# Score and state products cut into 32-row column tiles, with a new recorded order of the whole program

## The chip, the cores and the metric

The kernel runs on one core of one Trainium2 chip. The metric is the device time in microseconds (us) of one execution of the program. The kernel before takes 615.61 us, the median of 3 runs (615.38 to 616.79).

## The reference

Two stages stand one behind the other. The first is a linear recurrence over 768 time steps for 4 batches and 8 heads of width 48, with a complex decay per step and row; the second is a feed-forward network (FFN) over 3072 tokens, with a rational function between its two products. Cut to its core:

```python
mag = np.sqrt(a_re * a_re + a_im * a_im)
scale = np.minimum(mag, 0.999) / (mag + 1e-06)
a_re_n, a_im_n = (a_re * scale, a_im * scale)
for t in range(S):                                   # S = 768
    S_re, S_im = ar * S_re - ai * S_im + kv, ar * S_im + ai * S_re
    y[:, :, t] = np.einsum('bhd,bhde->bhe', q[:, :, t], S_re)
...
h = x @ w_in                                         # 3072 x 384 times 384 x 2048
P = a[0] + a[1] * h + a[2] * h2 + a[3] * h3
Q = 1.0 + np.abs(b[0]) * np.abs(h) + np.abs(b[1]) * h2
return ((P / (Q + 1e-06)) @ w_out).astype(np.float32)
```

Here kv is the outer product of row t of k and v, and h2, h3 are powers of h.

## The kernel before, in words

The recurrence is computed by chunks. Time is cut into 6 chunks of 128 steps; a unit is one chunk of one batch, so there are 24 units, taken in 12 pairs. For a unit, VectorE, ScalarE and GpSimd turn the decays into scaled rows of q and k (`norm`, `angle`, `trig`, `outer`): the last step there multiplies QK by the cosines (tile CO) and the sines (tile T) into two tiles Q, and a DMA through SyncE's queue then lays Q out as HQ, 96 rows for each head (48 real, 48 imaginary), with q in the first half and k in the second. Two HQ tiles take turns.

TensorE then does four things for a unit (`attn`). It transposes the k half (line 597). It multiplies k by q for each head, 128 x 128 scores over 96 rows (L608), four heads to a PSUM bank; VectorE multiplies them with a triangular mask into ST. It multiplies ST by V and the running state St by q (L624); these outputs have 32 rows each and use the array as four column tiles of 32 columns. And it updates the state from kT and V: in chunks 0 to 2 by eight products of 96 rows and 48 columns (L642), in chunks 3 and 4 by eight turned products with V's columns as rows (L653), whose result ScalarE evacuates, a DMA shifts, four transposes turn back (L663), and VectorE adds. The last chunk has no state to update. All banks of this stage come from a ring of two, `at`.

The FFN follows by tiles of 512 columns in `ph`: 96 of them, the first product at L704 and the second, into `po`, at L720. The first two pairs of units use plain float32 weights (4 bytes, two passes on TensorE for each product); all later ones use weights split into a high and a low part (wiH and wi, wh and wo), with three products for each. Between the two products stand some five operations each of ScalarE (Abs, Square, a reciprocal root) and VectorE, and a last one on VectorE or GpSimd (g). The weights come in as raw 8-byte numbers and are folded to float32 by VectorE, ScalarE and GpSimd at the start.

What runs when is not left to a scheduler at build time. Every operation is put into a plan, and a table, `ORDER`, holds a number for each of them: which operation comes next in the program, and on which engine it runs where there is a choice. So many multiplies may stand on VectorE or on GpSimd (lists `EN`, `DP`), and ScalarE's order says how often its function tables change between the sines and the FFN's functions. The planner's prices (`MM512`, the number ahead of each `pe` call) serve the search for an order; with a recorded one they have no effect on the program.

Until the first pair is there, `rouse` puts products on the idle array (L676), into a bank that nobody reads.

Of the kernel before, what the change touches and what calls it, by code (L numbers as in the profile page):

```python
# [221 lines left out]
def act(n, psum=False):  # L222
# [7 lines left out]
    "c-m!Hd3;XS+Fd8}AlW-ewP`ECt(I0P(*97ThKPCUH3db@LlE;&)I1XvgqA2Su9+f+nunXBt!injl9+qZ?2{PsW;)Ne&dc}v{`mfQUvKt4XYXfNYdy~c@I@G2"  # L230
    "MUjLcgx?qC6m|tIedfc}ClZDz{2}hI%CK-xo~p|BJ+Y7{K6n%Vl^jHiEni`3^!=<FT)ix{@T0sNQ!YDQUXQt(^%}BKT2j$h^7K0<5aTgLlF>{@n>9#MzuIq!"
    "Mv|Uud=QQYa#hz-yKlvp{DMPjvUwHx;)jRwhvca+<lDuvMS5bdJd_R58Ce@KLn<OG+AsS&>PDZ>j+G$%M9XY6RK+F?R!mQOsVPJ6{BT^JB2LcB6J6K5fnD+z"
    "F6iAd-$diCl;-{c^|9RvyQ7QD2~!I}F$vixC108&Jvu*Y7p^lVY0?{YVd;~m6l&<xrVfV6QeB*TqolpQVlJ!w#uqbiMr}6zbxk`_!eUCYHlZ47$`eUpL|S66"
    "DsPw4p~x^DaFKq@k`8Da-8;Jt4ob01;P*3C%dRg&u}|7*$JEw;iO#Fwq)QS{c`V^EU9-pNYo?9NL4JgP&OO;9&!jVIR{StCR(hd1MoK*2ZG{-0ys+)&F4vkd"
    "cbUvoQyi6lNgBW7(L;I6P&|`3ebh9CuRdhHR;TPEGG7W+u-%Qh>80|sGW2TG6HTQ^BG3_Mr7r%(UmjIxdg-+$!pbXuG&@0N;jBtC;nq&+j{iC*&=#Mms<y~j"
    "ER;!j<b+$vGEA0WILhL-a}b@eO>WcIZWUT*c7%e**@)KBem8@$QO>B@D)MH5?4Vy8qPy5TRbh5s`BmAo5Q;>Z%G1_h0j@h`tvPbrTIqC<SY6&8gd7RR-{n_i"
    "Pe5MyYq^hQj#xTTHOQ{)bIf@p_rs%dA32fMJ*S#=!-=pSI_3F^vF1uYqJ5d_XScPwI6kN+)vQ#xB=ZrBF;WGiF-->Jq#Pou3Zxvd-jgexWGU7V%dcS!Dq3Tm"
    "NW>FgDe8N>v3!a&8HFXp%{kO2s>)%bUQfg?CMKuw`%@fI*G-D`r(<EM%s>Nlm0;c4p3gh~_TEyv!i~)Ja$jaf+{xK1ooL@m3DIrrAgq&ds7-6q<d#%mK6XoA"
    "td@?*a2i?bWB_c5L{x=a5|H(PeEI;VWu2^JW<&6WOvGH70!?&G!+Ke)dfSW<R;j-BQ@)kN$X2wbg%7k#<a3!{AtiGlUa9aX)5r2e`()L@r_tYJpC=2WEA-Ah"
    "fSxMT?8HqOMJtBkbH?QoF*QM!;UwleOR=1OJyF3Z<Qqj&$jlT-0DKUH5)pYyB)-mjTFN$bN0h9=W$8+G{U`;PD)ZHwb}-(-R`n129WwbpnC>jXWcu0xw<TRE"  # L240
    "yF0G(-c;4g<mlJ!1Cl^YT8xiJeECFqD#(}UC5Poc8j))=l_QS4p4&t!VHLR?i$SWFT?yHI+DHb*GMd#;345eEu5kaVG+-QiU@H;$2~Rq!I+<3Cn}-ZONXzf)"
# [31 lines left out]


@with_exitstack
def attn_moe(ctx: ExitStack, tc: tile.TileContext, qk, aa, v, w_in, w_out, coef, heads, lanes, out):
    nc = tc.nc
    cst = ctx.enter_context(tc.tile_pool(name="cst", bufs=1))
    fast = ExitStack()
# [4 lines left out]


    ident = cst.tile([P, P], F32R, name="ident")
    cmask = cst.tile([P, P], F32, name="cmask")
    make_identity(nc, cmask)
    nc.scalar.activation(ident, cmask, AF.Copy)
    nc.gpsimd.memset(cmask, 0.25)  # L290
# [817 lines left out]
```

## Time and profile before

| | |
|---|---|
| median of the runs | 615.61 us |
| span of the profiled execution, first to last instruction | 612.9 us |
| TensorE products (PE) busy | 563.6 us, 92% |
| TensorE weight loads (PEld) busy | 482.3 us, 79% |
| VectorE (DVE) busy | 566.4 us, 92% |
| ScalarE (ACT) busy | 515.3 us, 84% |
| GpSimd (POOL) busy | 213.0 us, 35% |

The span is that of one profiled execution, the only time that the profile gives for it; the runs' median stands 2.7 us above it. Busy time counts a product from its start to its modelled end; since products are pipelined, their price is better read from one start to the next.

### The profile page before, as it was taken

Reading aid. Unit: us, or ns where it says so; the run is one execution under the profiler, and the core shown is the slowest. Engines: PE = TensorE matmul, PEld = TensorE weight load, DVE = VectorE, ACT = ScalarE, POOL = GpSimd, SP = SyncE. Lnnn points to the kernel's source line nnn. Section 1 sums busy time; section 2 is a strip of 40 time slices with the busy share of each in tenths; the row PEclk is TensorE's granted clock in tenths of the full one; section 3 lists DMA queues with packets and bytes.
Section 4 is the critical chain, followed back from the end, with each engine's and each line's share of the span. In section 5 each row is a group of like instructions: output and inputs, shape, how many; then the busy total and the mean of one; then the engine's idle time right before and its main releaser. Section 6 shows DMA issues by size and latency. Waiting matters only on the chain.

```text
span 612.9 us, 12009 instructions
## 1 busy us (share of the span) xinstructions
PE 563.6 (92%) x4454; PEld 482.3 (79%) x4454; DVE 566.4 (92%) x953; ACT 515.3 (84%) x867; POOL 213.0 (35%) x212
## 2 busy tenths in 40 slices
PE   0059999999999999999999999999999999999995
PEld 0038788888999999998878877878888888878874
DVE  8999999999999999999989999999999999778884
ACT  7979999999789889979988978989968877478781
POOL 2535346364536433515334133333520250000100
PEclk9999999999999999999999999999999999999999
DMA  8889632535573265155054255371423232010001
GB/s 286 312 218 314 141 96 69 133 100 140 104 155 102 46 126 135 53 105 129 6 138 104 64 123 116 97 164 19 101 78 113 54 63 32 1 52 1 1 2 56
DMA packets 40193, 63.57 MB, mean 104 GB/s; under 512 B 4544, under 2 KB 26176, under 8 KB 40128
## 3 DMA queue, kind: packets, MB, share of 16 engines
q1 hardware_dynamic: 39552, 62.08, 40.2%
q10 hardware_dynamic: 576, 0.66, 0.6%
q8 instruction: 37, 0.61, 0.4%
q14 instruction: 28, 0.23, 0.1%
HBM read 37.75 MB, written 4.72 MB: 69 GB/s over the span
## 4 chain that ended last, share of the span: by engine, by line
PE 49%; DVE 24%; ACT 14%; DMA 6%; issue 5%; SPq 1%; DVEq 0%; ACTq 0%
PE po L720 19%; PE ph L704 19%; DVE Af L336 5%; ACT Zf L351 4%; PE at L608 4%; PE at L624 4%; DVE g L336 4%; DVE T L336 3%; DVE ph L336 2%; DVE Q L336 2%; ACT Af L351 2%; DMA HQ<-Q 2%; PE at L597 1%; DVE MM L336 1%; DMA g<-in_w_out 1%
## 5 line engine op out<-in xcount | busy, mean ns | idle before, releaser
L720 PE MATMUL po<-g,wh 128*128 128x512 f32 (+1 forms) x576 | 167.2, 360 | 0.0
L704 PE MATMUL ph<-X,wiH 128*128 128x512 f32 (+1 forms) x576 | 144.2, 365 | 1.9 <-DVE Af L336 1.6
L720 PE MATMUL po<-g,wo 128*128 128x256 f32 (+1 forms) x462 | 141.2, 367 | 0.0
L720 PEld LDWEIGHTS po<-g,wh 128*128 128x128 f32 x576 | 102.9, 189 | 17.0 <-issue 1.2
L704 PEld LDWEIGHTS ph<-X,wiH 128*128 128x128 f32 x576 | 96.3, 188 | 21.2 <-DVE Af L336 2.9
L720 PEld LDWEIGHTS po<-g,wo 128*128 128x128 f32 x462 | 86.5, 189 | 12.1 <-issue 0.6
L336 POOL TENSOR_TENSOR g<-Af,Zf 128x512 fp32r<-128x512 f32 x31 | 42.4, 1366 | 148.2 <-DVE Af L336 63.9
L336 DVE SCALAR_TENSOR_TENSOR ph<-Zf,co,ph 128x512 f32<-128x512 f32 x96 | 71.8, 748 | 7.0 <-ACT Zf L351 3.8
L351 ACT ACTIVATE Zf<-ph,co 128x512 f32<-128x512 f32 x96 | 65.3, 680 | 14.6 <-DVE g L336 7.0
L351 ACT ACTIVATE Zf<-Af,co 128x512 f32<-128x512 f32 x80 | 57.8, 722 | 22.5 <-DVE ph L336 20.8
L336 DVE SCALAR_TENSOR_TENSOR g<-ph,co,Zf 128x512 fp32r<-128x512 f32 x80 | 59.5, 744 | 15.3 <-ACT Zf L351 14.6
L351 ACT ACTIVATE Af<-Af,co 128x512 f32<-128x512 f32 x96 | 68.8, 720 | 1.1
L704 PE MATMUL ph<-X,wi 128*128 128x512 f32 (+1 forms) x264 | 67.3, 358 | 0.0
L336 DVE SCALAR_TENSOR_TENSOR Af<-Af,co,g 128x512 f32<-128x512 f32 x80 | 64.7, 809 | 2.0
L351 ACT ACTIVATE Af<-ph 128x512 f32<-128x512 f32 x96 | 56.4, 589 | 8.0 <-PE ph L704 7.9
L336 DVE SCALAR_TENSOR_TENSOR Af<-ph,co,Af 128x512 f32<-128x512 f32 x80 | 59.7, 747 | 1.5
L704 PEld LDWEIGHTS ph<-X,wi 128*128 128x128 f32 x264 | 45.8, 188 | 8.1
L351 ACT ACTIVATE Zf<-Zf 128x512 f32<-128x512 f32 x80 | 50.3, 629 | 1.8
L608 PE MATMUL at<-HQ 96*128 96x128 f32 x384 | 49.5, 276 | 0.6 <-ACT kT L342 0.6
L608 PEld LDWEIGHTS at<-HQ 96*128 96x128 f32 x384 | 47.5, 191 | 2.9 <-ACT kT L342 1.3
L704 PE MATMUL ph<-wh,wi 128*128 128x256 f32 x192 | 45.0, 383 | 1.6 <-DVE g L336 1.6
L676 PE MATMUL po<-Q,cmask 128*128 128x256 f32 x28 | 10.0, 472 | 37.7 <-DVE Q L336 35.9
(213 smaller groups left out, 1053.9 us busy)
## 6 DMA issues: line engine op xcount, KB each, us to landing
HQ<-Q SPq DMA_DIRECT2D x141, 128.0 KB, 4.7
AA<-in_aa SPq DMA_DIRECT2D x23, 384.0 KB, 3.9
QK<-in_qk SPq DMA_DIRECT2D x23, 384.0 KB, 4.3
V<-in_v SPq DMA_DIRECT2D x24, 256.0 KB, 4.2
g<-in_w_in SPq DMA_DIRECT2D x6, 512.0 KB, 6.5
wh<-in_w_in SPq DMA_DIRECT2D x6, 512.0 KB, 5.8
wh<-in_w_out SPq DMA_DIRECT2D x8, 384.0 KB, 4.3
g<-in_w_out SPq DMA_DIRECT2D x8, 384.0 KB, 5.8
```

Of the source, the lines that this page charges most:

```text
L336: call = lambda e: getattr(e, kind)(*map(real, args), **{k: real(x) for k, x in kw.items()})
L351: e.activation(o(), i(), f, **kw)
L597: e.transpose(pt[:, i].bitcast(F32R), hq[:, 4 * g + i, 1, :], ident)
L608: e.matmul(pst[:, i, :], hf[:, 4 * g + i, 1, :], hf[:, 4 * g + i, 0, :], start=True, stop=True)
L624: e.matmul(py[32 * y:32 * y + 32, min(j, 2), :], l, sts[h // 4][:, h % 4, :] if q is None else hf[:, h, 0, :], start=q is None and j == 0, ...
L676: plan.op(dict(PE=(430, lambda e, x=x: e.matmul(idle[:, 0:2 * C], cmask, x(), start=True, stop=True)), SP=(0, lambda e: None)), (w,), ((id ...
L704: e.matmul(o, wt[f // 4 * NJ + j][:, f % 4 * P:f % 4 * P + P], moving(j, hl), start=n == 0, stop=n == len(prods) - 1)
L720: e.matmul(o[:, cols], wt[:, j * P:j * P + P], gg, start=(f == 0 and n == 0 and cols.start == 0), stop=(f == NFF - 1 and n == len(prods) - ...
```

## The change

Four things are changed. The scores of a head are no longer one product of 128 x 128, but four strips of 32 rows of k, each only with the columns of q from its first row on; heads are taken in pairs, and the odd head's strips lie in the bank in reverse order (`STRIPS`). The mask becomes one of two halves, in bfloat16, and V's odd heads have their blocks of 32 rows reversed on the host, so V has a second copy of these heads in plain order for the state. The state update is the same for all chunks: three products of 32 rows and 48 columns for each head; the turned products, their evacuation, DMA and transposes are gone. The two `at` banks are named outright. And there is another `ORDER`, with 32 warming products instead of 18 kept in it. Some planner prices differ too. `vn` serves a fallback path that does not run here.

```diff
-MM512 = 231.5
+MM512 = 236.5
-TURNED = 3
+VPAIR = VP + D
+VROW = H // 2 * (VPAIR + D)
+STRIPS = ((0, 1), (1, 2), (0, 0), (1, 3), (1, 1), (0, 2), (1, 0), (0, 3))
+def vcol(h):
+    return h // 2 * VPAIR + h % 2 * VP
 ORDER = (
-    "c-m!Hd3;XS+Fd8}AlW-ewP`ECt(I0P(*97ThKPCUH3db@LlE;&)I1XvgqA2Su9+f+nunXBt!injl9+qZ?2{PsW;)Ne&dc}v{`mfQUvKt4XYXfNYdy~c@I@G2"
+    "c-l=^33!#&ng0HpeIfq|1cyb*1;rN7I<_KJc%UON0t3n-7Qxg4VJGa1M3E&aAOWGsB0?ZQ0TqNs1)(ULBDS5WBLRnMAr}w?3OOf9$wIjQJMTFOoq6t)-20z<"
...
+    cmask = eye.bitcast(BF16).rearrange("p (y t) -> p y t", y=2)
...
+    banks = [ps.tile([P, 512], F32, name=f"at{i}") for i in range(2)]
...
-        u.V = V = buf(wk, [P, H * VP], F32, "V", VB)
+        u.V = V = buf(wk, [P, VROW], F32, "V", VB)
...
             def scores(e, g=g, pst=pst):
-                for i in range(4):
-                    e.matmul(pst[:, i, :], hf[:, 4 * g + i, 1, :], hf[:, 4 * g + i, 0, :], start=True, stop=True)
-
-            pe(870, scores, u.hq, (pst,))
+                for i in (0, 2):
+                    for y, q in STRIPS:
+                        h, s0 = 4 * g + i + y, 32 * (3 - q if y else q)
+                        e.matmul(pst[32 * q:32 * q + 32, i + y, s0:C], hf[:, h, 1, s0:s0 + 32], hf[:, h, 0, s0:C], start=True, stop=True)
+
+            pe(585, scores, u.hq, (pst,))
...
-        if c < TURNED:
-            def states(e):
-                for h in range(H):
-                    e.matmul(pd[0:96, h], kT[:, h], V[:, VP * h:VP * h + D], start=True, stop=True)
-            pe(1303, states, (V, kT), (pd,))
...
-            def turned(e):
-                for h in range(H):
-                    y, m = ((0, VP), (VP, D))[h % 2]
-                    e.matmul(pd[y:y + m, h // 2], V[:, VP * h:VP * h + m], kT[:, h], start=True, stop=True)
...
+        def states(e):
+            for h in range(H):
+                n = H // 2 * VPAIR + h // 2 * D if h % 2 else vcol(h)
+                for m in range(0, 2 * D, 32):
+                    e.matmul(pd[m:m + 32, h], kT[:, h, m:m + 32], V[:, n:n + D], start=True, stop=True)
+
+        pe(680, states, (V, kT), (pd,))
...
-                plan.op(dict(PE=(430, lambda e, x=x: e.matmul(idle[:, 0:2 * C], cmask, x(), start=True, stop=True)),
+                plan.op(dict(PE=(430, lambda e, x=x: e.matmul(idle[:, 0:2 * C], ident.bitcast(F32), x(), start=True, stop=True)),
```

TensorE's order at the scores of a unit, in the FFN's stretch of full 512-column tiles; a row's shape is weight columns x streamed columns. Before, eight heads stand between first-layer products:

```order
L704 MATMUL ph<-X_92,wiH_1070 128x512
L704 MATMUL ph<-X_92,wiH_229 128x512
L608 MATMUL at<-HQ_88 128x128 x8
L704 MATMUL ph<-X_92,wiH_348 128x512
L704 MATMUL ph<-X_92,wiH_1070 128x512
```

After, at a unit in the same place of the program, the last strips of such a stretch:

```order
L623 MATMUL at_112<-HQ_95 32x96 x2
L623 MATMUL at_112<-HQ_95 32x128 x2
L623 MATMUL at_112<-HQ_95 32x64 x2
L623 MATMUL at_112<-HQ_95 32x32 x2
L700 MATMUL ph<-X_99,wiH_310 128x512
L700 MATMUL ph<-X_99,wiH_337 128x512
```

Four full products of a group have become sixteen strips, and the stretch between full products is now one in column tiles.

The same engine at a state update. Before, in chunk 2, between first-layer products:

```order
L704 MATMUL ph<-X_92,wiH_1070 128x512
L704 MATMUL ph<-X_92,wiH_229 128x512
L642 MATMUL at<-V,kT 96x48 x8
L704 MATMUL ph<-X_92,wiH_348 128x512
L704 MATMUL ph<-X_92,wiH_1070 128x512
```

After, between products of the second layer and the first:

```order
L716 MATMUL po_3713<-g,wo-1_1196 128x512
L716 MATMUL po_3713<-g,wh_786 128x512
L661 MATMUL at_111<-V,kT 32x48 x24
L700 MATMUL ph<-X_99,wiH_334 128x512
L700 MATMUL ph<-X_99,wiH_374 128x512
```

Eight products of 96 weight columns are now twenty-four of 32, again a stretch of their own in column tiles.

GpSimd's order, some 115 instructions into its program, where units of the second and third chunk are prepared. Before:

```order
L336 TENSOR_TENSOR g<-Af,Zf 128x512
L336 TENSOR_TENSOR RU<-MM,RU 128x3x128
L336 TENSOR_TENSOR g<-Af,Zf 128x512
L336 COPY ncar<-MM 128x3
L336 TENSOR_TENSOR QK<-QK,RU 128x768
L336 TENSOR_SCALAR MM<-SQ 128x384
```

After:

```order
L350 TENSOR_TENSOR Q<-QK,T 128x768
L350 TENSOR_TENSOR RU<-MM,RU 128x3x128
L350 COPY ncar<-MM 128x3
L350 TENSOR_TENSOR QK<-QK,RU 128x768
L350 TENSOR_TENSOR Q<-QK,CO 128x768
L350 TENSOR_TENSOR wo_2485<-wo_676,wh_1816 128x384
```

Multiplies of 768 columns that VectorE did before (Q from QK and the sines or cosines) now stand on GpSimd, in the chain that ends in HQ.

## Rows read from the trace of the kernel before

**Rows 1.** The page: busy time by engine; busy tenths in 40 slices of 15.3 us.
```profile
PE 563.6 (92%) x4454; PEld 482.3 (79%) x4454; DVE 566.4 (92%) x953; ACT 515.3 (84%) x867; POOL 213.0 (35%) x212
...
PE   0059999999999999999999999999999999999995
...
DVE  8999999999999999999989999999999999778884
```

**Rows 2.** Waits of TensorE: who waited for whom, us in all, times, longest.
```profile
PE po L676 <- DVE Q L336: 35.9, 1, 35.9
PE ph L704 <- DVE g L336: 1.6, 2, 1.2
...
PE at L597 <- DMA HQ<-Q: 0.3, 1, 0.3
```

**Rows 3.** Table by stretch: length, busy us (instructions) by engine, PE clock, DMA share, GB/s.
```profile
60.00:120.00 60.00, 58.48 (x367) 50.91 (x365) 59.29 (x105) 57.94 (x101) 26.49 (x32) 1.00 0.47 117
240.00:300.00 60.00, 60.00 (x596) 55.00 (x595) 58.24 (x99) 54.47 (x94) 23.54 (x23) 1.00 0.34 77
480.00:540.00 60.00, 60.00 (x443) 49.11 (x442) 49.87 (x79) 42.03 (x68) 13.29 (x9) 1.00 0.22 38
```

**Rows 4.** Timeline of TensorE, 333 to 341 us: start, us, line, out<-in, rows*columns, shape, count.
```profile
333.33 1.05 PE L608 MATMUL at<-HQ 96*128 96x128 f32 x8
334.32 0.87 PE L653 MATMUL at<-kT,V 128*64 128x96 f32 x16
335.12 0.97 PE L704 MATMUL ph<-X,wiH 128*128 128x512 f32 x3
335.93 0.86 PE L704 MATMUL ph<-X,wi 128*128 128x512 f32 x3
336.62 0.86 PE L704 MATMUL ph<-X,wiH 128*128 128x512 f32 x3
337.41 1.08 PE L624 MATMUL at<-ST,V 128*32 128x128 f32 x32
338.31 1.06 PE L624 MATMUL at<-HQ,St 96*32 96x128 f32 x32
339.30 0.97 PE L704 MATMUL ph<-X,wiH 128*128 128x512 f32 x3
340.11 0.86 PE L704 MATMUL ph<-X,wi 128*128 128x512 f32 x3
```

**Rows 5.** Timeline of TensorE, a state update of an early chunk.
```profile
227.31 1.56 PE L642 MATMUL at<-V,kT 128*96 128x48 f32 x16
228.69 0.60 PE L704 MATMUL ph<-X,wiH 128*128 128x256 f32 x3
```

**Rows 6.** Timeline of TensorE, the transposes back of a later chunk.
```profile
291.57 0.41 PE L663 MATMUL at<-ident,kT 112*96 112x112 f32 x4
291.81 0.47 PE L704 MATMUL ph<-X,wiH 128*128 128x512 f32 x1
```

**Rows 7.** Chain that ended last, 38 to 45 us: start, us, what.
```profile
38.61 5.47 DMA HQ<-Q
```

**Rows 8.** Groups by shape: line, engine, operation, shapes, count; busy us, mean ns; idle before.
```profile
L336 DVE SCALAR_TENSOR_TENSOR Af<-Af,co,g 128x512 f32<-128x512 f32 x80 | 64.7, 809 | 2.0
L336 DVE SCALAR_TENSOR_TENSOR Af<-ph,co,Af 128x512 f32<-128x512 f32 x80 | 59.7, 747 | 1.5
L351 ACT ACT_TABLE_LOAD x15 | 19.2, 1283 | 0.3
L342 ACT ACTIVATE kT<-at 128x384 f32<-128x384 f32 x39 | 18.3, 485 | 6.4 <-PE at L597 6.4
L336 DVE TENSOR_TENSOR Q<-QK,T 128x768 f32<-128x768 f32 x18 | 17.8, 991 | 0.3 <-ACT T L550 0.2
L336 POOL TENSOR_TENSOR Q<-QK,T 128x768 f32<-128x768 f32 x5 | 9.9, 1976 | 13.9 <-ACT T L550 6.8 <-issue 6.0 <-DVE QK L336 1.1
```

**Rows 9.** Timeline of TensorE, 156.88 to 156.92 us.
```profile
156.89 0.32 PE L624 MATMUL at<-ST,V 128*32 128x128 f32 x4
```

More of the change, by code (lines that the diff above doesn't have):

```diff
@@ L286, in attn_moe @@
     ident = cst.tile([P, P], F32R, name="ident")
-    cmask = cst.tile([P, P], F32, name="cmask")
-    make_identity(nc, cmask)
-    nc.scalar.activation(ident, cmask, AF.Copy)
+    eye = cst.tile([P, P], F32, name="cmask")
+    make_identity(nc, eye)
+    nc.scalar.activation(ident, eye, AF.Copy)
+    cmask = eye.bitcast(BF16).rearrange("p (y t) -> p y t", y=2)
     nc.gpsimd.memset(cmask, 0.25)
-    nc.gpsimd.affine_select(out=cmask, in_=cmask, pattern=[[1, P]], compare_op=ALU.is_ge,
-                            fill=0.0, base=0, channel_multiplier=-1)
+    for q in range(4):
+        for y in range(2):
+            m = cmask[32 * q:32 * q + 32, y]
+            nc.gpsimd.affine_select(out=m, in_=m, pattern=[[1, P]], compare_op=ALU.is_ge,
+                                    fill=0.0, base=-32 * (3 - q if y else q), channel_multiplier=-1)
     smask = cst.tile([P, 2 * NJ, C], BF16, name="smask")
@@ L326, in buf, with at @@
         return Buf(plan, pool_, shape, dt, ring, bufs)
+    def at(*shape):
+        b = buf(ps, [P, 512], F32, "at", 2)
+        i, n = len(plan.rings["at"]) % 2, math.prod(shape)
+        b.make = lambda: banks[i][:, 0:n] if len(shape) == 1 else banks[i][:, 0:n].rearrange("p (a b) -> p a b", a=shape[0])
+        return b
     def dma(out_, in_, r, w, kb, hold=0, tail=2400, eng=("SP",)):
@@ L415, in shrink @@
         def shrink():
-            ways = dict(ACT=(act(n), lambda e: e.activation(part[:, 0:n], sign(), AF.Copy, scale=2.0 ** -112)), DVE=(dve(n, staged) + 61 * staged, down))
+            ways = dict(ACT=(act(n), lambda e: e.activation(part[:, 0:n], sign(), AF.Copy, scale=2.0 ** -112)), DVE=(dve(n, staged), down))
             if not staged:
@@ L436, in fold @@
         for f, to in ((first, part), (second, st)):
-            plan.op(dict(DVE=(dve(n) + 61 * staged, f)), (raw, part), (to,), port=not staged)
+            plan.op(dict(DVE=(dve(n), f)), (raw, part), (to,), port=not staged)
     def weights():
@@ L635, in attn @@
             return
[L636 to L668 removed]
+        sb = St[0:96, bb]
+        dst = bass.AP(sb.tensor, sb.offset, [sb.ap[0], [VPAIR, H // 2], [VP, 2], [1, D]])
+        pd = at(H, D)
+        def states(e):
[4 more added lines that the diff above has]
+        pe(680, states, (V, kT), (pd,))
+        mul(DM, lambda: dst, lambda: dst, lambda: pd[0:96].rearrange("p (g y) d -> p g y d", y=2), (pd, ("St", bb)), (("St", bb),), ALU.add, psum=True)
     def rouse(c, bb, many):
@@ L1076, in dense, with values @@
         return x.transpose(4, 0, 2, 3, 1, 5).reshape(NC, B, P, NJ, C)
-    def values(x):
+    def values(x, strips):
         x = x.reshape(B, H, NC, C, D).transpose(2, 0, 3, 1, 4).copy()
         x[..., 1::2, :] = np.roll(x[..., 1::2, :], 16, axis=-1)
-        return np.pad(x, [(0, 0)] * 4 + [(0, VP - D)]).reshape(NC, B, C, H * VP)
+        odd = x[..., 1::2, :].copy()
+        if strips:
+            x[..., 1::2, :] = odd.reshape(NC, B, 4, C // 4, H // 2, D)[:, :, ::-1].reshape(odd.shape)
+        x = np.pad(x, [(0, 0)] * 4 + [(0, VP - D)])
+        if not strips:
+            return x.reshape(NC, B, C, H * VP)
+        x = x.reshape(NC, B, C, H // 2, 2 * VP)[..., :VPAIR].reshape(NC, B, C, H // 2 * VPAIR)
+        return np.concatenate([x, odd.reshape(NC, B, C, H // 2 * D)], axis=-1)
     rows = np.arange(DM).reshape(H, D)
@@ L1089 @@
         "aa": np.stack([dense(inputs["a_re"]), dense(inputs["a_im"])], axis=3),
-        "v": values(inputs["v"]),
+        "v": values(inputs["v"], True),
+        "vn": values(inputs["v"], False),
         "w_in": inputs["moe_w_in"].view(np.int64)[rows],
```

130 lines of the change are left out of this document (55 added, 75 removed).

## The prediction

> **What bounds the kernel now.** I read the page first: busy time by engine, then its slices. TensorE (PE) is busy 563.6 us of a 612.9 us span and VectorE (DVE) 566.4 us; ScalarE (ACT) follows with 515.3 us and GpSimd (POOL) has 213.0 us [rows 1]. The slices show that PE begins late, after two empty slices of 15 us, and has hardly a free tenth from there to the end, while DVE is full from the start and thins out in the last quarter [rows 1]. So two engines are full at once, and the next view has to say which one waits. The list of waits of PE answers it: one wait of 35.9 us ahead of its first instruction, for DVE, and after it nothing above 1.6 us in all for one kind; the first layer's products (L704) wait 1.6 us for DVE, the transposes 0.3 us for the DMA of HQ [rows 2]. Once PE has started, it is hardly ever kept waiting: what it need not do should come off the end. The table by stretch qualifies that. From 60 to 120 us DVE is busy 59.3 us of 60 and ACT 57.9; from 240 to 300 us DVE has 58.2 and ACT 54.5; from 480 to 540 us DVE 49.9 and ACT 42.0, with PE at 60.0 [rows 3]. In the first half a shorter PE alone would soon run into DVE; the end is PE's alone. The clock granted to TensorE is 1.00 in each of these stretches, its level of 2.4 GHz [rows 3], so no term below carries a correction for it.
>
> **Scores.** A group of four heads is now four full products of 96 rows and 128 columns, each recorded twice, since float32 goes through in two passes. The eight records run from 333.33 to 334.32 us, and 0.10 of that is the entry into the column tiles that follow (below): 0.89 us, 0.111 for a record of 128 columns [rows 4]. The change cuts each head into four strips of 32 output rows, with 128, 96, 64 and 32 columns, and deals the strips of two heads to the four column tiles so that each gets 160 columns. What column tiles cost is in the trace already, for the value products (L624) use four of them: 32 records, eight rounds of four, go from 337.41 to 338.31 us [rows 4], 0.112 us for a round of 128 columns, the price of one full record. Four tiles run side by side at no loss, at 0.87 ns for a column and pass. A new group is two pairs of heads x 160 columns x 2 passes x 0.87 ns = 0.56 us, 0.33 less than now, and 48 groups save 16.0 us. That takes the tiles to run free of each other. If the four had to begin each step together, a pair would pay for rounds of 128 and 64 columns, twice each: 0.67 us a group, and the saving is 10.7. I take the free case, as the nearest row, the turned states (L653), is priced by the 96 columns that it streams though its two tiles load 64 and 48 weight columns, 112 if one held up the other.
>
> **States.** In the first three chunks eight products of 96 rows and 48 columns take 227.31 to 228.69 us, 1.38 us [rows 5], far more than their 16 x 48 x 0.87 ns = 0.67 us: each loads 96 weight columns twice, which at the same rate is 1.34. In strips of 32 rows on three tiles the loads are short and side by side and 0.67 us is left; 12 units save 8.5 us. In the two later chunks the turned products are 0.67 us of stream (8 rounds of 96 columns) and four transposes back take 291.57 to 291.81 us [rows 6]: 0.91 us against 0.67, and 8 units save 1.9 us. With them go eight evacuations and eight DMAs, for which nothing on PE was kept waiting [rows 2]. At the other end, a strip that took as long as its full product would leave no saving here.
>
> **Entries and exits, which the change adds.** A stretch in column tiles costs more than its products. Ahead of the values at 337.41 us the three first-layer products from 336.62 take 0.79 us, where the three from 335.93 take 0.69; the values last to 339.30, and the three products behind them take 0.81 [rows 4]. So 0.10 us of entry, 1.89 and 0.12 behind make 2.11 us for 16 rounds of 0.111, 1.78: 0.33 over. The turned states give the same: 0.10 us of entry, 0.80 and 0.12 behind are 1.02 us for 0.67, 0.35 over [rows 4]. I take 0.33 us for a stretch. PE's order before has 32 stretches in column tiles, 24 of values and 8 of turned states; the new one has 63, as scores, values and states mostly stand singly between FFN products. The 31 more cost 10.2 us (nothing, if they overlap with a neighbour after all). On PE 16.0 + 8.5 + 1.9 - 10.2 = 16.2 us are left. Fourteen more warming products on the idle array lie beside the 5.47 us of the DMA for which the first transposes wait [rows 7]; if that cover is gone they cost up to 6 us, at 0.43 for 256 columns in float32 (twice two records of 0.111).
>
> **The other engines.** By the order, eight multiplies Q<-QK,T and eight with CO leave DVE for POOL, with four of QK and five of Z: the sixteen alone are 16 x 0.99 = 15.9 us off DVE and 16 x 1.98 = 31.6 us on POOL [rows 8]. All rows together, each at its duration in this trace, take some 24 us off DVE. POOL, at 213 us, has the room, but there a multiply ends 1 us later, and so does the DMA behind it. What POOL costs DVE by running beside it is small so far: Af<-Af,co,g, on SBUF alone, has a mean of 0.809 us, its neighbour with a PSUM operand 0.747 [rows 8], 80 x 0.062 = 5 us in all; a quarter more POOL work makes it 6. ACT gets ten more table loads of 1.283 us, 12.8 us [rows 8], and loses seven evacuations of turned states, four of kT and some more of that size, 0.485 us each [rows 8], about 6: 7 us more on an engine that was idle for 97. V's DMA grows from 256 to 320 KB, issued well ahead; I cost it at nothing. That the order minds the delay between dependent neighbours earns no term: DVE has 232 of them after 227, ACT 184 after 185.
>
> **The sum.** DVE's relief, 24 us, is larger than PE's, so where DVE was the other full engine PE's saving should still come through: 612.9 - 16.2 = 596.7 us of span, and 2.7 more by which the median of the runs, 615.6, stands over the span: 599.4; I say 599.5 us. The ends of this case are 605 (tiles in step, 5.3 us less saved) and 590 (added stretches free); DVE's bound alone, 24 less, is 591.6.
>
> **Rivals.**
> First, slower: the feed of PE. The strips are short, and PE has to start a record each 0.56/32 = 17 ns in the scores and 0.67/48 = 14 ns in the states. The values start theirs each 28 ns (0.90 us for 32 [rows 4]), and no row shows a faster pace that is held. If 28 ns is the pace of the feed and not that of 128 columns, a group of scores costs 0.90 us and a state 1.35, the eight later ones lose 0.44 each, and with the stretches PE gets 0.5 - 0.4 + 3.5 + 10.2 = 13.8 us more: 629 us. It decides from about 22 ns a record: scores and states before are 48 x 0.89 + 12 x 1.38 + 8 x 0.91 = 66.6 us, less 10.2 for stretches, over 48 x 32 + 20 x 48 = 2,496 records. Against it: within 40 ns of time four records of the values begin [rows 9]. A burst is shown, a stream is not. Chance 0.09.
> By the Trainium skill, "TensorE: Matmul & The Clock Gate", section "Wait — 56ns, not 53.3ns?", the time from start to start never drops below about 25 ns, however few the columns; that would make the scores 0.80 us and a state 1.20, and the time by estimate 622 us. The trace's four starts within 40 ns speak against such a floor between column tiles; that it does not return in a stream of strips no run here shows.
> Second, slower: ACT takes over. If all of its 97 us of idle time were needed, 7 us more work would be 7 us more time, 622. Against it: from 480 to 540 us ACT has 18 of 60 us free, and from 60 to 120, where it has two, DVE has less still [rows 3]. Chance 0.04.
> Third, no change: multiplies of 2.0 us on POOL lengthen a unit's chain, only two HQ buffers run ahead, and PE's saving turns into waits for HQ and DVE: 613 to 617. Against it: PE waits 0.3 us for that DMA now [rows 2]. Chance 0.07.
> Fourth, more than forecast: the rows that the order puts on DVE ahead of the first mask multiply add up to some 9 us less by their durations in this trace, so PE's first attention may begin so much earlier and the end follow: 588 to 592. Against it, DVE at 59.3 of 60 us then feeds the first FFN tiles no faster. Chance 0.13.
>
> **How the numbers follow.** The forecast, 590 to 607 us, has 0.62; a smaller gain, up to 613, has 0.05. A measurement here can tell a change from none at about 0.3%, 1.8 us, so the lines run at 613.8 and 617.4. Faster: 0.62 + 0.05 + 0.13 = 0.80; same 0.07; slower 0.09 + 0.04 = 0.13. The range, 589 to 614, leaves out the feed, ACT, most of the third and a corner of the fourth, together 2 in 10; the forecast's own range is 590 to 607.
>
> **What would show it.** In the profile after, a group of scores between FFN products takes about 0.6 us and 0.3 for entry and exit, a state 0.7, read from start to start; there are 63 such stretches, and the three-product rows stay at 0.70 us. DVE is busy near 542 us, ACT near 522, POOL near 260, and PE's waits after its start stay at a few us. The forecast is wrong if the strips' records start no closer than 22 ns in the mean, if PE waits for more than 10 us for HQ, DVE or ACT once it has started, or if a stretch costs twice what the values pay.

## The result, and the profile after

The changed kernel takes 623.16 us, the median of 4 runs (620.78 to 626.14), beside 616.20 us of the kernel before on the same chip (615.38 to 618.09): a ratio of 1.012, with a 95% interval of 1.0079 to 1.016. It is slower, by about 7 us, where 599.5 was predicted. The profiled execution has a span of 621.0 us.

The page of the changed kernel: busy time by engine, three rows of the 40 slices (15.5 us each), and the shares of the chain that ended last. They answer to [rows 1].

```profile
PE 563.5 (91%) x6242; PEld 469.2 (76%) x6242; DVE 562.9 (91%) x929; ACT 522.3 (84%) x866; POOL 276.6 (45%) x251
...
PE   1268989899999999999999999999999999999995
...
DVE  8887999999999999999999998999998979788884
...
PEclk9977999999999999999999999999999999999998
...
PE 33%; DVE 29%; ACT 21%; issue 9%; DMA 5%; POOL 1%; SPq 1%; DVEq 0%; ACTq 0%; POOLq 0%
```

The chain of the kernel before, the same row of its page, which the prediction did not use:

```profile
PE 49%; DVE 24%; ACT 14%; DMA 6%; issue 5%; SPq 1%; DVEq 0%; ACTq 0%
```

PE's busy time is what it was, 563.5 after 563.6, since a busy PE also counts a product that is held up. DVE is down by 3.5 us where 24 were forecast; ACT is at 522.3, as forecast (522); POOL is at 276.6, not 260. Of the chain that ended last PE held 49% before and holds 33% now.

Waits of PE in the changed kernel, for [rows 2] (who waited for whom, us in all, times, longest). The 13.0 and 11.2 us at L672 lie among the warming products.

```profile
PE po L672 <- DVE wi L448: 13.0, 1, 13.0
PE po L672 <- DVE Q L350: 11.2, 1, 11.2
PE at L623 <- ACT kT L356: 7.3, 9, 2.2
PE ph L700 <- DVE Af L350: 5.3, 9, 1.1
PE ph L700 <- DVE g L350: 2.6, 3, 1.4
...
PE at L610 <- DVE St L350: 1.8, 3, 0.9
PE at L641 <- DVE ST L350: 1.6, 3, 1.3
```

With the warming products left out and all rows of the view added, an engine that waited 4.1 us for others after its start now waits 20.9, a little for everyone: ScalarE's kT, VectorE's Af, g, St, ST.

The table by stretch of the changed kernel, for [rows 3]; the first two rows are two short stretches of the head.

```profile
40.00:45.00 5.00, 3.19 (x97) 3.06 (x100) 2.80 (x5) 3.59 (x7) 2.99 (x5) 0.50 1.14 131
...
55.00:60.00 5.00, 4.89 (x12) 3.96 (x13) 4.79 (x9) 2.65 (x6) 3.54 (x4) 0.52 0.56 191
60.00:120.00 60.00, 55.89 (x562) 46.47 (x560) 57.42 (x96) 55.59 (x94) 30.42 (x33) 1.00 0.43 106
240.00:300.00 60.00, 55.72 (x968) 49.44 (x967) 56.16 (x96) 51.08 (x87) 28.42 (x24) 1.00 0.48 120
480.00:540.00 60.00, 60.00 (x597) 48.00 (x596) 51.65 (x86) 44.80 (x72) 20.76 (x14) 1.00 0.22 50
```

From 240 to 300 us PE has 4.3 us less of work in the 60 us than before, DVE 2.1 and ACT 3.4 less [rows 3]: no engine is full, and the work is not ahead for it. By the start of VectorE's step ph<-Zf,co,ph, FFN tile 16 (counted from 0) comes 4.3 us later than before, tile 32 7.8 and tile 95 8.1. Two stretches of the head are granted 0.50 and 0.52 of the clock, wholly or nearly the level of 1.2 GHz; the profiled execution of the kernel before has 1.00 in all of 40 to 65 us.

The products themselves are as cheap as they were meant to be. Timeline of PE in the changed kernel, the entry into column tiles, a state update and a group of scores, for [rows 4, 5]:

```profile
332.20 0.86 PE L700 MATMUL ph<-X,wiH 128*128 128x512 f32 x3
332.99 1.08 PE L641 MATMUL at<-ST,V 128*32 128x128 f32 x32
...
334.77 0.86 PE L661 MATMUL at<-V,kT 128*32 128x48 f32 x48
335.55 0.97 PE L700 MATMUL ph<-X,wiH 128*128 128x512 f32 x3
...
342.45 0.86 PE L700 MATMUL ph<-X,wiH 128*128 128x512 f32 x3
344.06 0.77 PE L623 MATMUL at<-HQ 96*32 96x96 f32 x32 [0.74 <-ACT kT L356]
344.75 0.50 PE L716 MATMUL po<-g,wh 128*128 128x512 f32 x1
```

From start to start a state takes 0.78 us with its exit (1.38 before [rows 5]), a group of scores 0.69 (0.99 [rows 4]). The three full products ahead of the values take 0.79, as they did before [rows 4]. But ahead of the scores PE stood 0.74 us for an evacuation on ACT: one such wait takes more than twice what one group saves, 0.30.

Groups by shape in the changed kernel, for [rows 8]:

```profile
L350 DVE SCALAR_TENSOR_TENSOR Af<-Af,co,g 128x512 f32<-128x512 f32 x80 | 72.9, 912 | 2.2
...
L350 DVE TENSOR_TENSOR Q<-QK,T 128x768 f32<-128x768 f32 x10 | 11.4, 1144 | 0.0
...
L350 POOL TENSOR_TENSOR Q<-QK,T 128x768 f32<-128x768 f32 x13 | 26.7, 2054 | 14.9 <-DVE QK L350 9.1 <-ACT T L564 5.4
```

The same 80 VectorE operations take 912 ns instead of 809, 8.2 us in all. Over all shapes of the two traces, fewer instructions took 23.3 us off VectorE (24 were forecast), and longer ones gave 16.4 back. The traces show where: Af<-Af,co,g takes 748 ns in the mean where no GpSimd instruction runs beside it (40 of the 80), and 1214 where one runs beside it for over nine tenths of its time (9). In the kernel before these are 746 ns (57 of 80) and 1112 (6): the price of one is much the same, and it falls due more often.

### The profile page after: what moved, and what is told of

The parts are those of the page before. It is cut to its first block, busy times and chain, and to the rows that moved or that the text cites. A ratio compares the mean times of both kernels' runs of the same rounds, so it can differ in the third digit from the quotient of the medians.

```text
span 621.0 us, 15656 instructions
## 1 busy us (share of the span) xinstructions
PE 563.5 (91%) x6242; PEld 469.2 (76%) x6242; DVE 562.9 (91%) x929; ACT 522.3 (84%) x866; POOL 276.6 (45%) x251
## 4 chain that ended last, share of the span: by engine, by line
PE 33%; DVE 29%; ACT 21%; issue 9%; DMA 5%; POOL 1%; SPq 1%; DVEq 0%; ACTq 0%; POOLq 0%
PE po L716 14%; PE ph L700 13%; DVE Af L350 9%; ACT Zf L365 7%; DVE g L350 6%; DVE ph L350 4%; ACT Af L365 3%; PE at L641 3%; PE at L623 2%; DVE T L350 2%; DVE ST L350 1%; ACT L365 1%; ACT SQ L365 1%; DVE Q L350 1%; DMA HQ<-Q 1%
## 5 line engine op out<-in xcount | busy, mean ns | idle before, releaser
L350 POOL TENSOR_TENSOR g<-Af,Zf 128x512 fp32r<-128x512 f32 x32 | 43.8, 1370 | 125.2 <-DVE Af L350 52.2
L350 DVE SCALAR_TENSOR_TENSOR Af<-Af,co,g 128x512 f32<-128x512 f32 x80 | 72.9, 912 | 2.2
L700 PE MATMUL ph<-wh,wi 128*128 128x256 f32 x192 | 48.0, 399 | 3.2 <-DVE g L350 2.6
L623 PEld LDWEIGHTS at<-HQ 96*32 96x32 f32 x1536 | 31.5, 112 | 18.6 <-ACT kT L356 9.9
L700 PEld LDWEIGHTS ph<-wh,wi 128*128 128x128 f32 x192 | 37.1, 199 | 10.2 <-DVE g L350 2.9
L623 PE MATMUL at<-HQ 96*32 96x64 f32 (+3 forms) x1536 | 35.6, 240 | 9.1 <-ACT kT L356 7.3
```

The lines of the kernel that those rows point to most:

```text
L350: call = lambda e: getattr(e, kind)(*map(real, args), **{k: real(x) for k, x in kw.items()})
L623: e.matmul(pst[32 * q:32 * q + 32, i + y, s0:C], hf[:, h, 1, s0:s0 + 32], hf[:, h, 0, s0:C], start=True, stop=True)
L700: e.matmul(o, wt[f // 4 * NJ + j][:, f % 4 * P:f % 4 * P + P], moving(j, hl), start=n == 0, stop=n == len(prods) - 1)
```

## The experiments

"Old order" is the sequence of the kernel before, "new order" that of the changed kernel; an order has two parts, the sequence and the engine of each movable operation. Ratios are to the kernel before, with 95% intervals. Cuts leave work out, as their expectations say.

**Products and order apart.** The first kernel has the change's products, mask and V layout, with the old sequence and engines.

```diff
 ORDER = (
-    the changed kernel's numbers
+    the numbers of the kernel before, without its 24 operations of the turned states
```

> The new products (strips for scores, three 32-row products a head for states, in all chunks) in the order and with the engine choices of the kernel before; only the three operations of each turned state update are left out. Theory A (the loss lies in the new order: 23 us moved from VectorE to GpSimd, of which 16 came back as longer VectorE operations, and a PE that waits): TensorE saves its 16 us with VectorE as loaded as before, so 600 to 609 us. Theory B (the products in column tiles cost more than their starts show): 620 us or more, as the changed kernel.

Measured: 617.1 us, ratio 0.9991 (0.9965 to 1.0018): no change, between the ranges of the two theories. So in the old order the new products bring nothing, and the 6 us from there to 623.16 come with the new order. Page and main waits of PE:

```profile
PE 555.9 (90%) x6214; PEld 462.0 (75%) x6214; DVE 566.2 (92%) x952; ACT 512.7 (83%) x860; POOL 215.8 (35%) x219
```

```profile
PE ph L703 <- DVE Af L353: 5.0, 9, 1.2
...
PE ph L703 <- DVE g L353: 2.2, 3, 1.0
PE at L613 <- DVE St L353: 2.0, 3, 1.3
```

DVE is where it was, 566.2. Each FFN tile's first VectorE step comes 2.0 to 2.4 us later than in the kernel before from tile 0 to tile 32, and 3.4 later at tile 95: TensorE's saving appears nowhere. I also summed, over PE's products and its stretches in column tiles, the time from start to start above the median of that kind (0.235 us for 512 columns of the first layer, and so on), where it is over 0.3 us and after the first 50: these gaps grow from 4.8 us to 19.9. With the smaller ones counted too they grow by some 20, but these hold the entries and exits, which were forecast. About 15 us were saved as work and spent as gaps.

The reverse: the new order with the old products; the mask and the host's layout of V follow them.

```diff
-                for i in (0, 2):
-                    for y, q in STRIPS:
...
+                for i in range(4):
+                    e.matmul(pst[:, i, :], hf[:, 4 * g + i, 1, :], hf[:, 4 * g + i, 0, :], start=True, stop=True)
...
-                for m in range(0, 2 * D, 32):
-                    e.matmul(pd[m:m + 32, h], kT[:, h, m:m + 32], V[:, n:n + D], start=True, stop=True)
+                e.matmul(pd[0:96, h], kT[:, h], V[:, n:n + D], start=True, stop=True)
```

> The changed kernel's order and engines, but four full products for a group of scores and eight of 96 rows for each state update, as the early chunks had before. Theory A (PE is no longer what bounds it under the new order): TensorE gets some 16 to 20 us more work, but much of it fills waits, so 625 to 633 us. Theory B (the strips cost): equal to the changed kernel or faster, 623 us or less. If PE still bounded it fully: 640 us.

Measured: 633.98 us, 1.0274 (1.0218 to 1.033). Here the products are worth some 11 us, 633.98 against 623.16 (9.5 by the ratios), though neither VectorE nor ScalarE is relieved: that they are worth nothing holds for the old order alone. The new order was made for them, and still loses: it costs 18 us with the old products and 6 with the new.

Then the two parts of the order crossed: the new sequence with the old choice between VectorE and GpSimd, and the old sequence with the new choice.

```diff
 ORDER = (
-    sequence and engines of one kernel
+    sequence of one kernel, VectorE or GpSimd as in the other
```

> The changed kernel in its own sequence, but each operation that may stand on VectorE or GpSimd stands where it stood before. Theory A1 (it is the engine choice: GpSimd beside VectorE stretches VectorE's operations): about 10 us faster than the changed kernel, 610 to 615 us, with Af<-Af,co,g back near 0.81 us. Theory A2 (it is the sequence, PE waiting for late masks, transposes and FFN tiles): within 3 us of the changed kernel or slower, 620 to 630 us, since VectorE has 23 us more to do in the same sequence.

> The new products in the sequence of the kernel before, but each operation that may stand on VectorE or GpSimd stands where the changed kernel has it. Theory A1 (engine choice): slower than with the old engine choice by 10 us or more, 612 to 622 us. Theory A2 (sequence): within 4 us of the old choice, 600 to 610 us.

Measured: 682.9 us, 1.1046 (1.0991 to 1.1101), and 656.49 us, 1.0635 (1.058 to 1.0691). Both crossings are far worse than either order and outside every range expected, so neither part can be judged without the other. The second has 24.9 us less VectorE work by count than the run with the new products in the old order, yet DVE is busier than there. Its page, two of its groups and two waits of PE:

```profile
PE 562.0 (86%) x6214; PEld 464.1 (71%) x6214; DVE 582.6 (89%) x924; ACT 514.3 (79%) x860; POOL 266.4 (41%) x247
```

```profile
L353 DVE SCALAR_TENSOR_TENSOR Af<-Af,co,g 128x512 f32<-128x512 f32 x80 | 68.6, 858 | 1.8
L353 DVE TENSOR_TENSOR_SCAN MM<-MM,ncar,SQ 128x128 f32<-128x128 f32 x69 | 44.5, 658 | 0.9 <-ACT SQ L359 0.9
```

```profile
PE ph L703 <- DVE Af L353: 16.5, 20, 2.9
PE at L664 <- DVE ST L353: 8.2, 4, 4.8
```

The scan in the kernel before:

```profile
L336 DVE TENSOR_TENSOR_SCAN MM<-MM,ncar,SQ 128x128 f32<-128x128 f32 x69 | 32.2, 479 | 0.1
```

Scans of 479 ns before take 658 ns here: 471 with no GpSimd instruction beside them (43 of 69), 1315 with one beside them for over nine tenths of their time (9). How the two engines' operations fall together decides what VectorE's cost.

**GpSimd by itself.** In the kernel before, each of the 31 multiplies g on GpSimd is followed by a second one whose result nobody reads.

```diff
     def emit(self, engines):
         self.ways[self.eng][1](engines[self.eng])
+        if self.extra and self.eng == "POOL":
+            self.extra(engines["POOL"])
```

> The kernel before, with each of GpSimd's 31 multiplies of g done twice in a row (the same product, written again), 42 us more GpSimd work and nothing else. Theory A1 (work on GpSimd stretches VectorE's operations on SBUF, and VectorE sets the time): VectorE's durations grow by 6 us or more and the time by 5 to 14 us, 622 to 631 us. Rival (GpSimd's work is hidden, as its idle time of 400 us suggests): 615 to 618 us.

Measured: 647.76 us, 1.0519 (1.0463 to 1.0574), more than any theory said. Two of its groups, and two waits of ACT:

```profile
L340 DVE SCALAR_TENSOR_TENSOR Af<-Af,co,g 128x512 f32<-128x512 f32 x80 | 70.6, 883 | 2.0
...
L761 POOL TENSOR_TENSOR g<-Af,Zf 128x512 fp32r<-128x512 f32 x31 | 46.6, 1505 | 2.4
```

```profile
ACT Zf L355 <- POOL g L761: 33.7, 24, 2.7
ACT Zf L355 <- DVE ph L340: 24.2, 36, 2.2
```

GpSimd, busy 35% of the span, is given 46.6 us more, and 31 us come out. Two prices show: VectorE's operations lengthen by 16.0 us over all shapes, and ACT waits 33.7 us (4.1 in the kernel before) for a buffer that GpSimd holds longer.

The changed kernel with work taken off GpSimd, and the control in the old order:

```diff
         mul(W, lambda: Z.t, lambda: MM.t, lambda: Z.t, (MM, Z), (Z,), eng=EN["e"])
+        third(lambda e: e.tensor_tensor(Z[:, 0], MM[:, 0], Z[:, 0], ALU.mult))
...
         mul(2 * W, lambda: QK.t, lambda: QK.t, lambda: RU.t, (QK, r0, r1), (QK,), eng=EN["qru"])
+        third(lambda e: e.tensor_tensor(QK[:, 0], QK[:, 0], RU[:, 0], ALU.mult))
```

> The changed kernel, with two multiplies of a unit's preparation (QK by RU, Z by MM) done on one of three 128-row parts where they stand on GpSimd: 15 and 19 instructions, of which two thirds are left out. GpSimd should lose about 34 us (15 x 1.91 and 19 x 1.17 us, two thirds), from 277 to about 243. Theory that the new order's 6 us over the old one are GpSimd's: through the stretching of VectorE's operations and the longer units' chains this should fall by 6 to 15 us, to 608 to 617, with Af<-Af,co,g back from 912 towards 860 ns. Rival, the order itself (its head, 40 to 60 us, and its sequence) costs the 6 us: 620 to 624.

> The control: the new products in the old order (617.1), with the same two multiplies cut to a third where they stand on GpSimd (11 and 14 instructions, about 25 us of its 216). If GpSimd's work costs time as such, whatever the order: 608 to 613, as much for each us as with the changed kernel. If GpSimd is only too much in the new order, where it has 61 us more: 615 to 617.

Measured: 616.71 us, 1.0006 (0.9982 to 1.003), and 614.64 us, 0.9968 (0.9936 to 0.9999). In the new order 33 us off GpSimd take 6.4 us off the time; in the old order 22 take off 2.5, hardly more than the measurement tells. Page and group of the first:

```profile
PE 562.1 (91%) x6242; PEld 468.8 (76%) x6242; DVE 558.4 (91%) x929; ACT 522.1 (85%) x866; POOL 243.8 (40%) x251
```

```profile
L350 DVE SCALAR_TENSOR_TENSOR Af<-Af,co,g 128x512 f32<-128x512 f32 x80 | 67.8, 847 | 2.2
```

DVE was not touched and its operation goes from 912 to 847 ns. The rival that the order's head alone costs the 6 us (620 to 624) falls; how much of the 6.4 is VectorE's stretching and how much the units' earlier results, the run does not part (over all shapes VectorE's durations give back 3.8 us).

**The clock in the head.** The new products in the old order, with another weight for the warming products:

```diff
-e.matmul(idle[:, 0:2 * C], ident.bitcast(F32), x(), start=True, stop=True)
+e.matmul(idle[:, 0:2 * C], eye, x(), start=True, stop=True)
```

> The new products in the old order, with the warming products' weights taken from the mask tile (dense numbers, as in the kernel before) in place of the identity. Theory C1 (the identity's zeros let the clock fall between 40 and 65 us): the granted clock is 1.00 there again and 2 us come back, 614 to 615.5 us. Theory C2 (the clock falls because the new products leave the array idle in a stretch that the old ones filled): the clock stays between 0.5 and 0.9 there, 616 to 618 us.

Measured: 616.54 us, 0.9992 (0.9962 to 1.0022), with 0.53 and 0.79 of the clock from 45 to 55 us. The zeros of the identity are not what lowers it. Nor are the new products: below, with VectorE's step cut in the kernel before, PE's first products are those of the kernel before, and the profiled execution has 0.76 and 0.56 of the clock from 45 to 55 us and starts tile 0 4.1 us late; with the new products and both cuts the clock is 1.00 from 40 to 65 us and tile 0 is 2.3 us late. The head differs from execution to execution, so 2 us there in one of them say nothing of the products. What lowers the clock was not found.

The clock is also a rival for the loss. Its mean over an execution is 0.976 to 0.988 in the four runs of the changed kernel; of 93 recorded executions of the kernel before, the 77 at 0.991 or above have a median of 616.1 us and the 16 below it 619.2. The changed kernel with work taken off GpSimd speaks against it: six of its executions at 0.976 to 0.980 have a median of 616.6 us, four at 0.990 to 0.992 have 616.9.

**Which engine bounds.** VectorE's step Af<-Af,co,g on a quarter of its columns, in the kernel before and with the new products in the old order:

```diff
-                stt(ta, ta, ks, hi, (a_, (g, 0), "co"), (a_,), psum=False)
+                cut = lambda f: lambda: f()[:, 0:128]
+                stt(cut(ta), cut(ta), ks, cut(hi), (a_, (g, 0), "co"), (a_,), psum=False)
```

> The kernel before, with one VectorE operation of each of the 80 split FFN tiles (Af<-Af,co,g) done on 128 of its 512 columns; the other columns of that step are left out. About 45 us of VectorE work go. Theory D (VectorE and TensorE bound it together): it falls to TensorE's own limit, 598 to 607 us. If VectorE alone bound it: 575 to 590 us. If ScalarE bound it: 613 to 617 us.

> The new products in the old order, with the same VectorE operation cut to 128 of its 512 columns. Theory D (TensorE's saving is real and was hidden by VectorE): 10 to 16 us below the kernel before with the same cut, 584 to 595 us. Theory B (the new products save nothing): equal to that kernel within 3 us.

Measured: 615.4 us, 0.9977 (0.9947 to 1.0007), and 612.69 us, 0.9924 (0.989 to 0.9959). Some 29 us less VectorE (45 were expected; the 128 columns still take 377 ns) moved the kernel before by nothing that can be told, which falls in the range given to ScalarE. The new products are 2.7 us ahead of it, within what their saving nothing allowed. The page of the kernel before with this cut, and two waits of DVE:

```profile
PE 563.9 (92%) x4454; PEld 485.2 (79%) x4454; DVE 537.2 (88%) x953; ACT 515.0 (84%) x867; POOL 205.5 (33%) x212
```

```profile
DVE g L336 <- ACT Zf L351: 20.6, 25, 2.3
DVE ph L336 <- ACT Zf L351: 12.5, 19, 1.6
```

The same two waits in the kernel before, and one of ACT there:

```profile
DVE g L336 <- ACT Zf L351: 14.6, 21, 1.5
DVE ph L336 <- ACT Zf L351: 3.8, 8, 1.1
```

```profile
ACT Zf L351 <- DVE ph L336: 20.8, 31, 2.0
```

DVE waits for ACT and ACT for DVE, many times for a microsecond. Each works for the other within one tile, so relief of one turns into waits for the other: the ring of the expectations. So ACT's square Zf<-Zf was cut to a quarter too, alone and with VectorE's step, with the old products and the new:

```diff
-            scal(AF.Square, 512, tz, tz, (z_,), (z_,), psum=whole)
+            part = tz if whole else (lambda b_=b_: b_.t[:, 0:128])
+            scal(AF.Square, 512, part, part, (z_,), (z_,), psum=whole)
```

> The kernel before, with the square Zf<-Zf of the 80 split FFN tiles done on 128 of its 512 columns only; the other three quarters of that step are left out. ScalarE should lose about 25 to 30 us (80 steps of 629 ns, of which about 0.25 to 0.3 us stays: an estimate from the 485 ns of a 384-column step). The step also stands in a tile's chain, which gets shorter by as much. Theory that three engines are coupled, none alone the bound: 608 to 615, a few us at most. Rival, ScalarE alone is what keeps the others waiting: 590 to 600. Rival, what is late is the preparation of units (HQ) and no tile: no change, 615 to 617.

> The new products in the old order (617.1 us) with the same cut of ScalarE's square to a quarter. TensorE and ScalarE are relieved here, VectorE is not. Coupled: 605 to 612, more than the same cut brings to the kernel before, and more than the cut of VectorE's step brought (612.7). ScalarE alone the bound: 590 to 600, as with the kernel before. TensorE's saving worth nothing at all: the same time as the kernel before with this cut.

> The kernel before with both cuts, VectorE's and ScalarE's. TensorE keeps all its work, 564 us busy. If TensorE is then the bound, 608 to 613, near its busy time and the 38 us before its first attention product and a few us of waits; if VectorE and ScalarE were what set the time before, 590 to 600.

> The new products in the old order, with both cuts: VectorE's step Af<-Af,co,g and ScalarE's square Zf<-Zf on 128 of 512 columns in the 80 split tiles. Here all three engines are relieved, so if they bound each other in a ring, TensorE's 16 us should come out: 594 to 604, at least 8 us below the kernel before with both cuts. If TensorE's saving is lost to something else (the head, the clock there, HQ), this is within 4 us of the kernel before with both cuts.

And both cuts in the 16 early tiles as well:

```diff
-                stt(ta, ta, 2.0, tz, (a_, z_), (a_,), ALU.subtract, 0)
+                cut = lambda f: lambda: f()[:, 0:128]
+                stt(cut(ta), cut(ta), 2.0, cut(tz), (a_, z_), (a_,), ALU.subtract, 0)
```

> The control of the run with all relief: the kernel before with both cuts in the 80 split tiles (612.0) and the same cuts in the 16 early ones. With the new products this gave 604.6. If TensorE's saving is worth something only where the other two engines are relieved, this stays at TensorE's own work, 608 to 612, and the products are worth 4 to 7 us here, against none without relief. If the products are worth nothing even so: 603 to 606.

> The new products in the old order with both cuts (608.8), and the same two engines relieved in the first 16 tiles too, those with plain weights: ScalarE's square Zf<-Zf and VectorE's step Af<-Af,Zf there on 128 of 512 columns. Until tile 16, 170 us into the program, no relief has moved anything so far: the tile stands 2 us later than in the kernel before whatever was cut. If the FFN's steps on VectorE and ScalarE set the pace there as well, the tile comes 5 to 10 us earlier and the end with it: 598 to 604. If the units' preparation or the folding of the weights sets it, tile 16 stands where it was: 607 to 609.

| relieved, all in the old order | old products, us and ratio | new products, us and ratio |
|---|---|---|
| nothing | 616.2, 1 | 617.1, 0.9991 (0.9965 to 1.0018) |
| VectorE | 615.4, 0.9977 (0.9947 to 1.0007) | 612.69, 0.9924 (0.989 to 0.9959) |
| ScalarE | 613.42, 0.9948 (0.9919 to 0.9977) | 612.39, 0.9955 (0.9924 to 0.9987) |
| both | 611.99, 0.9926 (0.9898 to 0.9954) | 608.77, 0.989 (0.9841 to 0.994) |
| both, early tiles too | 609.46, 0.9906 (0.989 to 0.9923) | 604.62, 0.9797 (0.9747 to 0.9847) |

No engine alone is the bound: 29 us off VectorE, 23 off ScalarE or 16 off TensorE are worth at most 3 us. "ScalarE alone" (590 to 600) falls. Row by row the new products' lead is -0.9, 2.7, 1.0, 3.2 and 4.8 us by the medians (0.6, 3.3, -0.4, 2.2 and 6.7 by the ratios); only in the last row do the two intervals part. Both cuts were to bring the new products to 594 to 604 and 8 us ahead if the ring held TensorE's whole saving; 608.77 and 3.2 are what the rival said, a saving lost to something else. So the ring of these two steps explains a part of it. From tile 0 to tile 16 the early cut takes 3.3 us off with the new products and 2.0 with the old, less than the 5 to 10 expected, so the FFN's engines set some of the pace there too. The chain of the last row, old products first, then new:

```profile
PE 88%; DMA 4%; DVE 3%; ACT 3%; issue 1%; SPq 0%; ACTq 0%; DVEq 0%
```

```profile
PE 66%; DVE 13%; ACT 11%; DMA 4%; issue 4%; POOL 1%; SPq 0%; ACTq 0%; DVEq 0%; POOLq 0%
```

With the old products and everything relieved, PE holds 88% of the chain: in the old order only now is it near to what the prediction took it for, and only now are shorter products worth something clear of the noise. The share alone does not tell it, though. The old products with ScalarE alone relieved, then in the new order:

```profile
PE 72%; DVE 16%; ACT 5%; DMA 3%; issue 2%; SPq 1%; POOL 0%; ACTq 0%; DVEq 0%
```

```profile
PE 44%; DVE 24%; ACT 10%; issue 7%; DMA 4%; POOL 1%; SPq 1%; DVEq 0%; ACTq 0%; POOLq 0%
```

At 72% the new products are worth nothing that can be told, at 44% some 10 us. With everything relieved some 7 of the 16 us still stay in gaps (7.7 us of them against 0.9, by the same sum as above), 3.1 of them at the states; the old sequence was laid out for longer products. Whether one made for them, with the old engines, would get these back was not tried.

**The new order under the same reliefs.**

> The changed kernel with both cuts: VectorE's Af<-Af,co,g and ScalarE's Zf<-Zf on 128 of 512 columns in the 80 split tiles. In the old order these two brought 617.1 down to 608.8. If the engines of the FFN ring set the pace in the new order as well, the same 8 us or more: 611 to 615. If GpSimd's queue and the units' preparation set it, less than 4 us: 619 to 623.

> The changed kernel with three reliefs: the two multiplies of a unit's preparation cut to a third where they stand on GpSimd, and VectorE's and ScalarE's steps cut to a quarter in the 80 split tiles. One by one the first took 6.4 us off and the other two together 9.5. If they are separate losses, 606 to 608, and the new order then ties with the old one under the same two cuts (608.8), so that GpSimd's work was its whole loss. If they overlap, 610 to 613, and something of the new order is left unexplained.

Measured: 613.64 us, 0.9954 (0.992 to 0.9987), and 609.1 us, 0.9904 (0.9875 to 0.9932). The FFN's two cuts take 9.5 us off, as they take 8.3 off in the old order; GpSimd's on top another 4.5, less than the 6.4 it gave alone, so the two losses overlap in part. With all three the new order is where the old one is with two (608.77); the old one with all three was not run. That fits GpSimd's added work as the main part of what it loses; it does not prove that it is all. Of the kernels that compute everything none was faster than the kernel before.

## Why the prediction was wrong, point by point

- Scores, states, entries and exits: right. A group takes 0.69 us with its exit where 0.6 and some exit were forecast, a state 0.78 where 0.7 was; 15 us of gaps at an unchanged time say that about 15 us of work did go. One count was off: the kernel before has 27 stretches in column tiles, not 32, since five of the eight turned updates stand directly beside values; 36 are added, for 11.9 us, and 14.5 us are left in place of 16.2. The rival of the feed, 28 or 25 ns a record, is out: 32 records in 0.69 us are at most 22 ns each in the mean, 48 in 0.78 some 16. By the Trainium skill, "TensorE: Matmul & The Clock Gate", section "Wait — 56ns, not 53.3ns?", starts come no closer than about 25 ns; between column tiles this trace differs, and the measurement decides.
- The step that failed is the sum: "DVE's relief, 24 us, is larger than PE's, so where DVE was the other full engine PE's saving should still come through". It rests on the reading that an engine which hardly waits gives back whatever it need not do, and it gives the new order no cost of its own. In its place the runs showed two things. In the old order 16 us off PE are worth 0 and 29 off DVE nothing that can be told; with VectorE and ScalarE both relieved in all tiles PE's 16 are worth 5 to 7, so these engines hold each other for that part, and for the rest the cause stays open. And the new order costs 6 us with the new products; 33 us less GpSimd work gives 6.4 back. The prediction's own sign, over 10 us of waits after PE's start, came true with 20.9. That PE's few waits [rows 2] mean work placed just behind that of the others is how I read it, not something tested.
- "some 24 us off DVE": the count was right (23.3, though seven multiplies with CO moved and not eight), the durations were not. "A quarter more POOL work makes it 6" put the stretching of Af<-Af,co,g at 1 us more; it was 8.2, and 16.4 over all shapes.
- POOL's room: "POOL, at 213 us, has the room" judged it by its busy share. The doubled multiplies cost 31 us of time for 46.6 of work.
- ACT's 7 us more: right in size, 522.3. By number the rival that ACT takes over, 622, comes nearest to the measured time; that is luck, since 23 us off ACT were worth 3 us in the old order.
- "Two engines are full at once, and the next view has to say which one waits" was a false choice. The third rival, PE's saving turning into waits, was the nearest in kind, at 613 to 617 and a chance of 0.07; it looked at HQ's DMA, and the waits are for kT, Af and g. That the new order would lose a further 6 us had no rival.
- "The clock granted is 1.00": true of the stretches read. The new head has stretches at 0.50, which the sum had no term for; the runs do not show that they cost time.

## What to carry to other kernels

Few waits on an engine do not show that its saving reaches the end: where its neighbours wait for each other tile by tile, a shorter engine can buy gaps. Its share of the chain that ended last does not settle it either (49% and 72% with nothing gained, 44% with some 10 us). Test it by cutting a step of each engine, alone and together; a bound shows as a cut that pays alone. Where every operation's place is on record for the old durations, test the new products in the old order before judging either. And price a move to GpSimd by what it does to its neighbours' durations and to the buffers it holds, not by its idle share.

## What the runs showed of the hardware

- Some SBUF operations of VectorE stretch with GpSimd's work beside them: Af<-Af,co,g 809 ns at 213 us of GpSimd, 847 at 243.8, 883 at 258.5, 858 at 266.4 (the second crossing) and 912 at 276.6. In these five traces the ones with no GpSimd instruction beside them take 746 to 749 ns in the mean, the ones with one beside them for over nine tenths of their time 979 to 1214. The scan went from 479 to 658 ns in one crossing; g<-Af,Zf hardly moved, 709 ns before and 724 in the changed kernel. Operations with a PSUM operand kept their time: ph<-Zf,co,ph has 749 ns in the changed kernel and 750 with the doubled multiplies.

```profile
L350 DVE SCALAR_TENSOR_TENSOR ph<-Zf,co,ph 128x512 f32<-128x512 f32 x96 | 71.9, 749 | 11.7 <-ACT Zf L365 9.1 <-ACT Af L365 2.2
```

```profile
L340 DVE SCALAR_TENSOR_TENSOR ph<-Zf,co,ph 128x512 f32<-128x512 f32 x96 | 72.0, 750 | 24.5 <-ACT Zf L355 18.6 <-ACT Af L355 5.6
```

- Products of 32 weight columns on separate column tiles start at most 16 to 22 ns apart in the mean.
- The granted clock fell to 0.50 from 40 to 45 us of the changed kernel, where PE was busy 3.19 of the 5 us; in the kernel before PE was busy the same 3.19 us there at 1.00. In another run with the same first products it fell to 0.56 from 50 to 55 us, PE busy all 5.00. Why was not settled.
